# Moving a load of x ahead of the R and V weights in the head of a fused convolution and channel-mix kernel

One core of a Trainium2 chip. The metric is the time of one execution in microseconds of device time (us), lower is better.

## The reference

The kernel computes two layers, one after the other, on x of shape 8 x 4160 x 192 (fp32):

```python
# 1: causal convolution, 7 taps, weights shared by the 24 channels of a head (8 heads)
w = softmax(weight, axis=-1)                       # [8, 7]
y[b, s, h, :] = sum_k w[h, k] * x_pad[b, s + k, h, :]
# 2: channel mix
y_prev = y shifted by one position (zeros first)
xk = mu_k * y + (1 - mu_k) * y_prev
xr = mu_r * y + (1 - mu_r) * y_prev
k  = relu(xk @ w_k)                                # w_k: 192 x 1024
out = sigmoid(xr @ w_r) * ((k * k) @ w_v)          # w_v: 1024 x 192
```

## The kernel before

x is taken two batches at a time, in groups of blocks of 120 positions. A group is loaded to bf16 by a casting DMA from POOL (the GpSimd queue), convolved on the matrix engine (PE) as a product with a banded matrix `toe` that VectorE (DVE) makes from the softmax, copied out of PSUM by ScalarE (ACT), transposed, and mixed on DVE; then K products, ReLU (ACT), square (DVE), R products, sigmoid (ACT), V products, product with the sigmoid (DVE), store. PSUM is one ring of four tiles for everything. The program sets the order on each engine itself (`manual_schedule`). `tails` are two tiles for the last 64 positions of a batch, zeroed on POOL; SP (SyncE) issues the loads of mu.

Only the head changes. Its core, with cuts:

```python
def softmax():
    nc.vector.tensor_reduce(out=w_max, in_=w_raw, ...)     # waits for the attention weights
    ...
    nc.scalar.activation(out=w_exp, in_=w_exp, func=AF.Exp)
    for s in range(2):
        nc.scalar.copy(out=xbs[0][...], in_=x_f32[...])    # first group's x to bf16
    nc.scalar.activation(out=w_sig, ..., func=AF.Sigmoid)  # loads the sigmoid table (1.28 us at 7.56)
    ...

def k_section(ns):                                         # first bundle:
        run(first, 0)                                      # second group's transposes
        warm(k_ps[0], 2)
        for n in ns: k_mm(n, True, True)                   # high 128 channels
        for n in ns: k_mm(n, False, False)                 # low 64 channels
    # ... (the later bundles)

def prologue():
    # ... attention weights and first group's x on the SP and ACT queues
    masks_band()                         # two masks on POOL
    load_x(1)
    load_wk(0, NF // 2)                  # three DMAs
    # ... warm-up products, softmax
    make_toe()
    load_wk(NF // 2, NF)                 # three DMAs
    load_x(2)
    load_wr()                            # five DMAs
    load_wv()
    # ... six tiny loads of mu on the SP queue
    for t in tails:
        nc.gpsimd.memset(t, 0.0)
    conv(0, 0)
    conv(1, 0)
    tr_first()                           # first group's transposes, its mix for K
    x_tile(3, nc.vector)
    load_x(3)                            # fourth group's x
```

Of the kernel before, what the change touches and what calls it, by code (L numbers as in the profile page):

```python
# [14 lines left out]
def kernel(  # L15
# [17 lines left out]
    P = 128  # L33
# [137 lines left out]

    tails = [const.tile([P, 2, 2, P], BF16, tag=f"tail{i}", name=f"tail{i}") for i in range(2)]

    def load_wk(f0, f1):
        fs = slice(f0 * P, f1 * P)
        nc.gpsimd.dma_start(out=wk[:, 0, fs], in_=moe_w_k[0:P, fs])
        nc.gpsimd.dma_start(out=wk[0:LO, 1, fs], in_=moe_w_k[P:D, fs])
        nc.gpsimd.dma_start(out=wk[LO:P, 1, fs], in_=moe_w_k[P:D, fs])

    def load_wr():  # L180
        nc.gpsimd.dma_start(out=wr[:, 0, :], in_=moe_w_r[0:P, :])
        for i in (1, 2):
            nc.gpsimd.dma_start(out=wr[0:LO, i, :], in_=moe_w_r[P:D, :])
        for i in (1, 3):
            nc.gpsimd.dma_start(out=wr[LO:P, i, :], in_=moe_w_r[P:D, :])

    def load_wv():
        nc.gpsimd.dma_start(out=wv, in_=moe_w_v.rearrange("(f p) d -> p f d", p=P))

    def softmax():  # L190
        nc.vector.tensor_reduce(out=w_max, in_=w_raw, axis=mybir.AxisListType.X, op=ALU.max)
        nc.vector.tensor_tensor(
            out=w_exp, in0=w_raw, in1=w_max.unsqueeze(2).to_broadcast([P, H, K]), op=ALU.subtract
        )
        nc.scalar.activation(out=w_exp, in_=w_exp, func=AF.Exp)
        xbs[0] = three.tile([P, GB, 2, D], BF16, tag="xb", name="xb")
        for s in range(2):
            nc.scalar.copy(out=xbs[0][:, : groups[0][2], s, :], in_=x_f32[:, :, s, :])

        nc.scalar.activation(out=w_sig, in_=w_exp[:, 0, 0:1], func=AF.Sigmoid)  # L200
        nc.vector.tensor_reduce(out=w_sum, in_=w_exp, axis=mybir.AxisListType.X, op=ALU.add)
        nc.vector.reciprocal(out=w_sum, in_=w_sum)
        nc.vector.tensor_tensor(
            out=w_nrm,
            in0=w_exp,
            in1=w_sum.unsqueeze(2).to_broadcast([P, H, K]),
            op=ALU.mult,
        )
# [18 lines left out]
    def make_toe():  # L227

        m = mod8[:, :]
        nc.vector.tensor_tensor(  # L230
            out=w_all,
            in0=w_nrm.unsqueeze(2).to_broadcast([P, H, 8, K]),
            in1=bass.AP(tensor=m.tensor, offset=m.offset, ap=[m.ap[0], [0, H], [1, 8], [1, K]]),
            op=ALU.mult,
        )
        with nc.allow_low_precision(reason="a sum of one number and zeros"):
            nc.vector.tensor_reduce(
                out=w_per,
                in_=w_all,
                axis=mybir.AxisListType.X,  # L240
                op=ALU.add,
            )
        for h0, h1 in ((0, 3), (3, H)):
            n = h1 - h0
            nc.vector.tensor_tensor(
                out=toe[:, h0:h1, :].rearrange("p h (c r) -> p h c r", r=8),
                in0=w_per[:, h0:h1, :].unsqueeze(2).to_broadcast([P, n, P // 8, 8]),
                in1=band.rearrange("p (c r) -> p c r", r=8).unsqueeze(1).to_broadcast([P, n, P // 8, 8]),
                op=ALU.mult,
            )  # L250
# [28 lines left out]
    def conv_small(g, copies):  # L279


        nb = groups[g][2]
        ys[g] = [two.tile([P, 4, P], BF16, tag=f"y_small{i}", name="y_small") for i in range(3)]
        tiles = [ring.tile([P, 2, BANK], FP32, tag="k", name="ps_c") for _ in range(2)]
        banks = [t[:, i, 0 : nb * P] for t, i in ((tiles[0], 0), (tiles[1], 0), (tiles[0], 1))]
        for i, o in enumerate(banks):
            o = o.rearrange("p (n s c) -> p n s c", n=nb, s=2 if i == 2 else 1)
            c0, c1 = (P, D) if i == 2 else (0, P)
            for h in range(c0 // G, -(-c1 // G)):
                a, b = max(c0, h * G), min(c1, h * G + G)  # L290
                nc.tensor.matmul(
                    out=o[:, :, :, a - c0 : b - c0],
                    lhsT=toe[:, h, :],
                    rhs=xbs[g][:, :nb, slice(0, 2) if i == 2 else slice(i, i + 1), a:b],
                    start=True,
                    stop=True,
                )
        for i, o in enumerate(banks):
            copies[i](out=ys[g][i][:BLK, :nb, :].rearrange("p n c -> p (n c)"), in_=o[:BLK, :])
# [140 lines left out]
    def k_mm(n, hi, start):  # L440


        s, j = slots[n]
        L = steps[s][2]
        xk = xks[s]
        if start and n not in k_ps:
            k_ps[n] = ring.tile([P, 2, BANK], FP32, tag="k", name="ps_k")
        ps = k_ps[n]
        nf = STEP // L

        for f in range(nf):
            fs = slice((j * nf + f) * P, (j * nf + f + 1) * P)
            for i in range(2):
                r = slice(0, P) if hi else slice(i * LO, (i + 1) * LO)
                nc.tensor.matmul(  # L455
                    out=ps[:, i, f * L : (f + 1) * L],
                    lhsT=wk[r, 0 if hi else 1, fs],
                    rhs=xk[r, i if hi else 2, :L],
                    start=start and f == 0,
                    stop=not start and f == nf - 1,  # L460
                )

    def k_section(ns):

        s, _ = slots[ns[0]]
        if steps[s][2] == TAIL:
            return k_mm_tail(ns[0], steps[s][0])
        if ns[0] == 0:

            k_ps[0] = ring.tile([P, 2, BANK], FP32, tag="k", name="ps_k")  # L470
            run(first, 0)
            warm(k_ps[0], 2)
            for n in ns:
                k_mm(n, True, True)
            for n in ns:
                k_mm(n, False, False)
            return
        h = len(ns) // 2 if ns[0] > 2 else len(ns)
        for n in ns[:h]:
            k_mm(n, True, True)  # L480
        for n in ns[:h]:
            k_mm(n, False, False)
        for n in ns[h:]:
            k_mm(n, False, True)
        for n in ns[h:]:
            k_mm(n, True, False)
# [150 lines left out]
    def conv(g, c):  # L637
        if g < 3:
            act_, dve_ = nc.scalar.copy, nc.vector.tensor_copy
            return conv_small(g, (act_, dve_ if g < 2 else act_, act_))  # L640
        conv_mm(g, c)
        for k in range(c, min(c + 2, len(chunks(g)))):
            conv_out(g, k, nc.scalar.copy)
# [53 lines left out]
    def run(table, b):  # L697
        for fn, a in table.get(b, ()):
            fn(*a)

    def warm(ps, n):
        for i in range(n):
            nc.tensor.matmul(out=ps[:, i % 2, :], lhsT=ones_t, rhs=zeros, start=True, stop=True)

    def prologue():
        nc.sync.dma_start(
            out=w_raw,
            in_=bass.AP(tensor=weight.tensor, offset=weight.offset, ap=[[0, P], [K, H], [1, K]]),
        )
        nc.vector.memset(x_f32[0:32, 0, :, :], 0.0)  # L710
        nc.vector.memset(ones_t, 1.0)
        load_x_first(0, nc.sync)
        load_x_first(1, nc.scalar)
        nc.scalar.preload_act_table(AF.Exp)
        nc.vector.memset(zeros, 0.0)
        x_tile(1, nc.vector)
        nc.gpsimd.affine_select(
            out=ident,
            in_=ones_t,
            pattern=[[1, P]],  # L720
            compare_op=ALU.is_equal,
            fill=0.0,
            base=0,
            channel_multiplier=-1,
        )
        masks_band()
        load_x(1)
        load_wk(0, NF // 2)

        warm(ring.tile([P, 2, BANK], FP32, tag="k", name="warm"), WARM)  # L730
        x_tile(2, nc.vector)
        nc.vector.memset(wr[:, 2:4, :], 0.0)
        masks_mod8()
        softmax()
        make_toe()
        load_wk(NF // 2, NF)
        load_x(2)
        load_wr()
        load_wv()
        for i, m in enumerate((moe_mu_k, moe_mu_r)):  # L740
            nc.sync.dma_start(out=mu[:, i, 0:1], in_=m[0:P])
            nc.sync.dma_start(out=mu[0:LO, i, 1:2], in_=m[P:D])
            nc.sync.dma_start(out=mu[LO:P, i, 1:2], in_=m[P:D])
        for t in tails:
            nc.gpsimd.memset(t, 0.0)
        conv(0, 0)
        conv(1, 0)
        tr_first()
        x_tile(3, nc.vector)
        load_x(3)  # L750

    with tc.manual_schedule():
        prologue()
# [52 lines left out]
```

## Time and profile before

| | |
|---|---|
| timed runs before the change was tried | 445.12, 445.36, 445.37 us |
| the profiled execution | 447.0 us, span 445.3 us, mean granted clock 0.995 (share of PE's full clock) |
| PE busy | 97% of the span |
| x and weights loaded on the POOL queue until about 37 us | the DMA engines 90% busy or more in 30 of the 32 us from 4 to 36 |

The views that matter are the chain of waits (what released each step), the stretches (busy time by engine and granted clock) and ScalarE's timeline (in brackets the idle time ahead of a piece, and what ended it); the prediction shows their lines.

### The profile page before, as it was taken

The page shows a single profiled execution, that of the slowest core. Times are in us where ns is not written, and L with a number is a line of the kernel's source. Part 1 is how long each engine was busy: PE and PEld are TensorE (multiplying, and loading weights), DVE is VectorE, ACT ScalarE, POOL GpSimd, SP SyncE. Part 2 cuts the span into 40 slices and gives each one's busy share as a digit, 9 for nine tenths or more (in the row PEclk, how much of TensorE's full clock was granted, in tenths as well). Part 3 has the DMA queues.
Part 4 walks back from the last instruction along what each step waited for, and adds up shares of the span by engine and source line. Part 5 has one row for each costly group of instructions (what it writes and reads, how often), then busy time and mean ns, then how long its engine had stood idle before and what let it go on. Part 6 is the DMA issues. An engine that isn't in the chain of part 4 may idle for free.

```text
span 445.3 us, 9733 instructions
## 1 busy us (share of the span) xinstructions
PE 430.9 (97%) x3888; PEld 304.9 (68%) x3951; DVE 388.3 (87%) x700; ACT 354.1 (80%) x461; POOL 47.0 (11%) x69
## 2 busy tenths in 40 slices
PE   7789999999999999999999999999999999999996
PEld 3455766766867766776676776677676677666776
DVE  5969799889988999889989888889988898999973
ACT  5868888888897797888888788888889778777772
POOL 6750001102020100012020010010200000000000
PEclk9989999999999999999999999999999999999999
DMA  8996858989596693294899494466955553421123
GB/s 132 147 188 129 199 147 159 152 200 184 133 205 172 146 204 85 79 206 130 161 214 163 116 228 126 111 99 179 195 144 133 158 124 113 102 82 63 45 72 117
DMA packets 133545, 63.94 MB, mean 144 GB/s; under 512 B 84071, under 2 KB 133499, under 8 KB 133499
## 3 DMA queue, kind: packets, MB, share of 16 engines
q1 hardware_dynamic: 95014, 48.38, 41.0%
q0 software_dynamic: 37696, 14.39, 27.7%
q8 instruction: 31, 0.51, 0.4%
q10 hardware_dynamic: 788, 0.54, 0.4%
q14 instruction: 16, 0.12, 0.1%
HBM read 29.39 MB, written 36.99 MB: 149 GB/s over the span
## 4 chain that ended last, share of the span: by engine, by line
PE 86%; DVE 4%; ACT 3%; DMA 3%; issue 2%; POOL 1%; DVEq 0%; ACTq 0%
PE ps_v L554 37%; PE ps_k L455 36%; PE ps_r L549 4%; PE ps_r L550 4%; PE ps_c L271 4%; DMA xb<-in_x_dram 3%; ACT y L313 2%; DVE k L525 1%; ACT k_sb L506 1%; DVE o_sb L581 1%; PE ps_vt L554 1%; ACT r_sb L571 0%; ACT y L316 0%; DVE xr L436 0%; DVE d L392 0%
## 5 line engine op out<-in xcount | busy, mean ns | idle before, releaser
L506 ACT ACTIVATE k_sb<-ps_k 128x1024 bf16<-128x1024 f32 x260 | 245.9, 1037 | 14.5 <-PE ps_k L455 11.2
L455 PE MATMUL ps_k<-xk,wk 64*128 64x512 bf16 (+3 forms) x994 | 189.3, 375 | 5.8 <-ACT k_sb L506 0.6
L554 PEld LDWEIGHTS <-k 128*128 128x128 bf16 x2048 | 170.9, 98 | 14.4 <-issue 0.3
L554 PE MATMUL ps_v<-wv,k 128*128 128x192 bf16 x2048 | 179.4, 246 | 0.1
L525 DVE TENSOR_TENSOR k<-k_sb 128x1024 bf16<-128x1024 bf16 x256 | 167.9, 685 | 10.3 <-ACT k_sb L506 9.2
L455 PEld LDWEIGHTS <-wk 64*128 64x128 bf16 (+1 forms) x1056 | 67.0, 96 | 102.7 <-issue 58.8
L581 DVE TENSOR_TENSOR o_sb<-ps_v,r_sb 128x768 f32<-128x768 f32 x63 | 60.2, 955 | 23.7 <-PE ps_v L554 23.2
L571 ACT ACTIVATE r_sb<-ps_r 128x768 bf16<-128x768 f32 x64 | 53.1, 830 | 24.8 <-PE ps_r L550 24.8
L313 ACT CAST y<-ps_c 120x480 bf16<-120x480 f32 (+4 forms) x78 | 36.1, 518 | 32.4 <-PE ps_c L271 32.4
L122 POOL DMA_DIRECT2D xb<-in_x_dram x34 | 30.7, 908 | 173.7 <-PE ps_k L455 95.2
L549 PE MATMUL ps_r<-wr,xr 128*128 128x192 bf16 x256 | 47.5, 246 | 0.2 <-DVE o_sb L581 0.2
L550 PE MATMUL ps_r<-wr,xr 128*128 128x192 bf16 x256 | 47.6, 247 | 0.0
L436 DVE TENSOR_TENSOR xr<-xr,yT 128x1024 bf16<-128x1024 bf16 (+1 forms) x66 | 36.2, 549 | 2.3
L436 DVE TENSOR_TENSOR xk<-xk,yT 128x1024 bf16<-128x1024 bf16 (+1 forms) x64 | 35.5, 555 | 2.2
L392 DVE TENSOR_TENSOR d<-yT 128x1536 bf16<-128x1536 bf16 (+4 forms) x38 | 31.7, 835 | 0.1
L271 PE MATMUL ps_c<-xb,toe 128*128 128x480 bf16 (+2 forms) x120 | 28.6, 338 | 2.0 <-DMA xb<-in_x_dram 2.0
L433 DVE TENSOR_SCALAR xk<-d,mu 128x1024 bf16<-128x1024 bf16 (+1 forms) x64 | 27.2, 425 | 1.1
L550 PEld LDWEIGHTS <-xr 128*128 128x128 bf16 x256 | 25.1, 98 | 3.9 <-issue 0.4
L549 PEld LDWEIGHTS <-xr 128*128 128x128 bf16 x256 | 25.0, 98 | 3.5
L433 DVE TENSOR_SCALAR xr<-d,mu 128x1024 bf16<-128x1024 bf16 (+1 forms) x66 | 27.1, 410 | 0.0
L316 ACT CAST y<-ps_c 120x480 bf16<-120x480 f32 (+4 forms) x41 | 18.9, 509 | 8.0 <-PE ps_c L271 8.0
L271 PEld LDWEIGHTS <-toe 128*128 128x128 bf16 x120 | 10.9, 98 | 3.0 <-issue 2.2
(69 smaller groups left out, 89.7 us busy)
## 6 DMA issues: line engine op xcount, KB each, us to landing
out_dram<-o_sb SPq DMA_DIRECT2D x61, 384.0 KB, 2.7
y_dram<-y SPq DMA_DIRECT2D x10, 900.0 KB, 6.9
xb<-in_x_dram POOLq DMA_DIRECT2D x14, 480.0 KB, 8.3
xb<-in_x_dram POOLq DMA_DIRECT2D x6, 432.0 KB, 8.2
xb<-in_x_dram POOLq DMA_DIRECT2D x10, 192.0 KB, 6.4
y_dram<-y SPq DMA_DIRECT2D x3, 450.0 KB, 4.1
y_dram<-y SPq DMA_DIRECT2D x1, 810.0 KB, 5.6
xb<-in_x_dram POOLq DMA_DIRECT2D x2, 384.0 KB, 8.7
```

The source lines that it names most:

```text
L271: nc.tensor.matmul(out=ps[:, :, :, i * G : (i + 1) * G], lhsT=toe[:, h, :], rhs=xbs[g][:, :nb, :, h * G : (h + 1) * G], start=True, stop=True,
L313: copy(out=yh[:, :, :, c0 : c0 + n], in_=ps[:BLK, :, :, 0:n])
L433: nc.vector.tensor_scalar(out=o, in0=d[:, sl, :L], scalar1=mu[:, i, part : part + 1], scalar2=None, op0=ALU.mult)
L436: nc.vector.tensor_tensor(out=o, in0=o, in1=yT[:, sl, c0 : c0 + L], op=ALU.add)
L455: nc.tensor.matmul(out=ps[:, i, f * L : (f + 1) * L], lhsT=wk[r, 0 if hi else 1, fs], rhs=xk[r, i if hi else 2, :L], start=start and f == ...
L506: nc.scalar.activation(out=k_sb, in_=ps.rearrange("p a b -> p (a b)"), func=AF.Relu)
L525: nc.vector.tensor_tensor(out=o, in0=i, in1=i, op=ALU.mult)
L549: nc.tensor.matmul(out=o, lhsT=hi, rhs=wr[:, 0, :], start=True, stop=False)
L550: nc.tensor.matmul(out=o, lhsT=lo, rhs=wlo, start=False, stop=True)
L554: nc.tensor.matmul(out=o, lhsT=k2s[s][:, f, t * P : (t + 1) * P], rhs=wv[:, f, :], start=(f == 0), stop=(f == NF - 1),)
L571: nc.scalar.activation(out=r_sbs[s, j], in_=ps, func=AF.Sigmoid)
L581: nc.vector.tensor_tensor(out=o_sb.rearrange("p (b t) d -> p b (t d)", b=2), in0=v_ps.pop((s, j)), in1=r_sbs.pop((s, j)), op=ALU.mult,)
```

## The change

The intent is to end PE's 2 us wait for the fourth group's x, and to start the first K product earlier. The diff, cut to its core:

```diff
-    def load_wk(f0, f1):                    # halves of the columns, 2 x 3 DMAs
+    def load_wk():                          # all columns, 3 DMAs
     ...
     def load_wr():                          # 5 DMAs become 3
     ...
         nc.scalar.activation(out=w_exp, in_=w_exp, func=AF.Exp)
+        nc.scalar.activation(out=w_sig, in_=w_exp[:, 0, 0:1], func=AF.Sigmoid)
         ... copies of the first group's x ...
-        nc.scalar.activation(out=w_sig, in_=w_exp[:, 0, 0:1], func=AF.Sigmoid)
     ...
     def make_toe():                         # whole w_all, w_per, then toe in 3 + 5 heads
+        hc = -(-P // G)                     # now all three steps for 6 heads, then for 2
     ...
-            run(first, 0)
-            warm(k_ps[0], 2)
+            warm(k_ps[0], 3)
             for n in ns:
                 k_mm(n, True, True)
+            run(first, 0)
             for n in ns:
                 k_mm(n, False, False)
     ...
-            return conv_small(g, (act_, dve_ if g < 2 else act_, act_))
+            return conv_small(g, (act_, dve_ if g == 0 else act_, act_))
     ...
+        load_x(1)
         masks_band()
-        load_x(1)
-        load_wk(0, NF // 2)
+        load_wk()
     ...
-        load_wk(NF // 2, NF)
         load_x(2)
-        load_wr()
-        load_wv()
         ... mu ...
-        for t in tails: ...
         conv(0, 0)
-        conv(1, 0)
         tr_first()
+        conv(1, 0)
         x_tile(3, nc.vector)
         load_x(3)
+        load_wr()
+        load_wv()
+        for t in tails: ...
```

More of the change, by code (lines that the diff above doesn't have):

```diff
@@ L172 @@
     tails = [const.tile([P, 2, 2, P], BF16, tag=f"tail{i}", name=f"tail{i}") for i in range(2)]
-    def load_wk(f0, f1):
-        fs = slice(f0 * P, f1 * P)
-        nc.gpsimd.dma_start(out=wk[:, 0, fs], in_=moe_w_k[0:P, fs])
-        nc.gpsimd.dma_start(out=wk[0:LO, 1, fs], in_=moe_w_k[P:D, fs])
-        nc.gpsimd.dma_start(out=wk[LO:P, 1, fs], in_=moe_w_k[P:D, fs])
+    def load_wk():
+        nc.gpsimd.dma_start(out=wk[:, 0, :], in_=moe_w_k[0:P, :])
+        nc.gpsimd.dma_start(out=wk[0:LO, 1, :], in_=moe_w_k[P:D, :])
+        nc.gpsimd.dma_start(out=wk[LO:P, 1, :], in_=moe_w_k[P:D, :])
     def load_wr():
         nc.gpsimd.dma_start(out=wr[:, 0, :], in_=moe_w_r[0:P, :])
-        for i in (1, 2):
-            nc.gpsimd.dma_start(out=wr[0:LO, i, :], in_=moe_w_r[P:D, :])
-        for i in (1, 3):
-            nc.gpsimd.dma_start(out=wr[LO:P, i, :], in_=moe_w_r[P:D, :])
+        lo = bass.AP(tensor=moe_w_r.tensor, offset=moe_w_r.offset + P * D, ap=[[D, LO], [0, 2], [1, D]])
+        nc.gpsimd.dma_start(out=wr[0:LO, 1:3, :], in_=lo)
+        nc.gpsimd.dma_start(out=wr[LO:P, 1:4:2, :], in_=lo)
     def load_wv():
@@ L229, in make_toe @@
         m = mod8[:, :]
-        nc.vector.tensor_tensor(
-            out=w_all,
-            in0=w_nrm.unsqueeze(2).to_broadcast([P, H, 8, K]),
-            in1=bass.AP(tensor=m.tensor, offset=m.offset, ap=[m.ap[0], [0, H], [1, 8], [1, K]]),
-            op=ALU.mult,
-        )
-        with nc.allow_low_precision(reason="a sum of one number and zeros"):
-            nc.vector.tensor_reduce(
-                out=w_per,
-                in_=w_all,
-                axis=mybir.AxisListType.X,
-                op=ALU.add,
-            )
-        for h0, h1 in ((0, 3), (3, H)):
-            n = h1 - h0
+        hc = -(-P // G)
+        for h0, h1 in ((0, hc), (hc, H)):
+            n = h1 - h0
+            nc.vector.tensor_tensor(
+                out=w_all[:, h0:h1],
+                in0=w_nrm[:, h0:h1, :].unsqueeze(2).to_broadcast([P, n, 8, K]),
+                in1=bass.AP(tensor=m.tensor, offset=m.offset, ap=[m.ap[0], [0, n], [1, 8], [1, K]]),
+                op=ALU.mult,
+            )
+            with nc.allow_low_precision(reason="a sum of one number and zeros"):
+                nc.vector.tensor_reduce(
+                    out=w_per[:, h0:h1, :],
+                    in_=w_all[:, h0:h1],
+                    axis=mybir.AxisListType.X,
+                    op=ALU.add,
+                )
             nc.vector.tensor_tensor(
@@ L743, in prologue @@
             nc.sync.dma_start(out=mu[LO:P, i, 1:2], in_=m[P:D])
+        conv(0, 0)
+        tr_first()
+        conv(1, 0)
+        x_tile(3, nc.vector)
+        load_x(3)
+        load_wr()
+        load_wv()
         for t in tails:
             nc.gpsimd.memset(t, 0.0)
-        conv(0, 0)
-        conv(1, 0)
-        tr_first()
-        x_tile(3, nc.vector)
-        load_x(3)
     with tc.manual_schedule():
```

## The prediction

> **What bounds the kernel now.** I read the page first, then the chain that ended last over the first 40 us, then the waits over the rest, then stretches with the granted clock, then ScalarE's timeline.
>
> The page says that the matrix engine is busy nearly everywhere but in the first two slices, 22 us:
>
> ```profile
> span 445.3 us, 9733 instructions
> PE 430.9 (97%) x3888; PEld 304.9 (68%) x3951; DVE 388.3 (87%) x700; ACT 354.1 (80%) x461; POOL 47.0 (11%) x69
> PE   7789999999999999999999999999999999999996
> ```
>
> All that the change touches is over by about 31 us. From 36 us on the waits view, asked for PE alone, has two lines, together 0.8 us in over 400: what is won or lost at the head should go through to the end at about one to one.
>
> ```profile
> PE ps_k L455 <- ACT y L313: 0.6, 1, 0.6
> PE ps_r L549 <- DVE o_sb L581: 0.2, 1, 0.2
> ```
>
> So the question is the head alone. The chain of waits, cut to 12 to 37 us (start, duration, what):
>
> ```profile
> 14.32 0.59 POOL tail L745
> 14.91 0.34 issue
> 15.25 0.58 POOL xb L122
> 15.83 0.35 issue
> 16.18 7.10 DMA xb<-in_x_dram
> 23.28 0.14 issue
> 23.41 0.98 PE ps_c L271 x8
> ...
> 28.43 0.69 ACT k_sb L506
> 29.12 0.22 issue
> 29.34 1.04 ACT k_sb L506
> 30.38 0.04 issue
> 30.42 2.80 PE ps_v L554 x32
> ```
>
> The reader is to see that the fourth group's x, issued on POOL at 15.25 behind two memsets of the tails, lands at 23.28, and that its convolution (L271) starts only then. After it the chain hangs on ScalarE's ReLU, which frees the PSUM tile for the first V product.
>
> The stretches view shows what that wait also does to the clock (columns: PE, PE load, DVE, ACT, POOL busy, granted clock, DMA, GB/s):
>
> ```profile
> 21.40:23.40 2.00, 0.00 (x0) 0.02 (x1) 1.97 (x5) 1.63 (x2) 1.59 (x3) 1.00 1.45 170
> 23.40:24.74 1.34, 1.33 (x15) 1.30 (x16) 1.31 (x4) 0.72 (x2) 1.34 (x2) 1.00 1.53 176
> 24.74:28.16 3.42, 3.42 (x16) 1.14 (x14) 2.12 (x5) 2.65 (x6) 1.05 (x3) 0.50 1.60 193
> ```
>
> PE is empty for 2.0 us and then runs 3.42 us at half clock: its waiting costs twice.
>
> ScalarE's timeline tells how much of this is worth anything (start, busy, what, idle before):
>
> ```profile
> 14.12 3.77 ACT L506 ACTIVATE k_sb<-ps_k 128x1024 bf16<-128x1024 f32 x4 [2.19 <-PE ps_k L455]
> 17.75 1.60 ACT L299 CAST y_small<-ps_c 120x512 bf16<-120x512 f32 x3
> 19.17 3.86 ACT L506 ACTIVATE k_sb<-ps_k 128x1024 bf16<-128x1024 f32 x4
> 24.02 1.35 ACT L313 CAST y<-ps_c 120x480 bf16<-120x480 f32 x3 [0.99 <-PE ps_c L271]
> ...
> 27.51 3.77 ACT L506 ACTIVATE k_sb<-ps_k 128x1024 bf16<-128x1024 f32 x4 [0.77 <-PE ps_k L455]
> ```
>
> From 14.12 to 23.03 ScalarE has no gap: it, and not PE, sets the pace there. It then idles 0.99 us for the late convolution and 0.77 us for the K products at half clock.
>
> [...] The trace has one such stretch of 3.42 us; the window before it, 21.33 to 24.74, was 41% busy (1.4 of 3.41 us)[...]. [...] the trace has 1283 ns for the second one, at 7.56. [...] the two 480 KB loads of the fifth group land at 25.8 and 28.5, which is 2.7 us for 480 KB with packets of 384 bytes, and these queues are 90% busy or more from 16 to 36 us. I use the measured rate, about 180 KB a us.
>
> **The change, part by part.**
>
> 1. *x of the fourth group ahead of R and V weights.* Now 144 KB of R and 384 KB of V stand before it, and the tails' memsets[...]. After: groups two and three (384 KB each), K (512 KB), then this x (480 KB). The third group landed at 14.6 (issue 10.1 plus 4.5); 480 KB more at 180 KB a us is 2.7 us, so 17.3 us instead of 23.28. Its convolution cannot be wanted before about 20.9 (part 4). The wait of 2.0 us on PE and the 0.99 us on ScalarE go. With no gap I expect the half clock to go too, and with it the 0.77 us of ScalarE. Sum on the path: 1.76 us.
>
> 2. *Who pays: R and V.* Bytes in front of R grow by 480 KB: landing 15.7 plus 2.7 is about 18.4; first use 24.1 now, about 22.6 then. V: 18.6 plus 2.7 is 21.3; first use 30.4 now, about 28 then. Both have some 4 to 6 us to spare. The fifth group's x has the same bytes in front of it as before, and its issue on POOL comes no later; landing at 28.5 or earlier, use at 33.1 minus 2.4.
>
> 3. *Fewer loads.* K in 3 instead of 6 issues, R in 3 instead of 5. Bytes are the same; POOL saves 5 issues of about 0.57 us, and the third group's x no longer waits for a free semaphore (1.75 and 0.27 us before its two issues). It shortens a stream that is bound by the DMA engines: nothing on the path by itself.
>
> 4. *First transposes ahead of the second convolution; toe by heads; sigmoid table early.* Now: first K product at 12.72, first ReLU at 14.12. After, in steps. The table load moves to 5.3, ahead of the two casts of x, so the casts end at 8.0 instead of 7.54; the first convolution starts at 8.13 anyway, behind the warm-up products. Six heads of the toe matrix: 0.62 and 0.62 us times 6/8, plus about 0.6 for 768 elements, ready at 7.7; the last two by 8.4, used at 8.9. ScalarE's first copy then starts at 8.5 instead of 8.97 and its second ends at 9.6; the nine transposes (0.64 us) end at 9.95 instead of 10.94. On DVE: yT copy 0.50, difference 0.43, mix 0.75, from 9.6: the first K product at about 11.4, 1.3 us earlier. But the start of the ReLU gets less: the eight K products take about 1.0 us (12.4), then the second group's transposes, now between the halves, 0.8 us (13.2, their inputs are cast on ScalarE by 12.0), then the low halves 0.45 us: ReLU at 13.65, 0.5 us earlier. The low half also needs the last mu load, which landed at 12.4 (5.76 plus 6.6), and the K weights (12.5): no limit at 13.2, but close. Worth 0.5 us.
>
> 5. *Copies.* The second group's third copy moves from DVE (0.69 us) to ScalarE, ahead of the first ReLU: in ScalarE's idle 2.19 us, free. One warm-up product more, in a gap: free.
>
> Sum: 0.5 at the first ReLU, 0.99 before the casts, 0.77 before the third set of ReLUs: 2.26. A second way to the same place: after, ScalarE is full from 13.65. Until the casts: 8.91 us of work, 22.55; casts and sigmoid 2.73 us, 25.3; two ReLUs and the third, ending 2.85 us later, free the tile of the V product: about 28.1 instead of 30.42, 2.3 us earlier. From there on PE is full. 445.36 minus 2.3 is 443.1; I say 443.0, as the DMA stream also loses its stall at 14.5 to 16.
>
> **Rivals.**
>
> *A: PE's loss is the measure.* PE idles 2.0 us, loses about 1.7 us at half clock, and starts 1.3 us earlier: up to 5 us, 440.4. Against it: ScalarE's gapless run from 14.12 to 23.03 stands in between, with all four PSUM tiles in its hands. I give it little.
>
> *B: the K weights, in fewer and larger loads, or mu, become the new wait.* The high part of K now brings all 1024 columns before any low part. If low parts land at 13 or later, part 4 gives nothing: 443.6. For it: everything lands 5.8 to 6.4 us after issue in that crowded stretch. Against: 512 KB are the same bytes, issued from about 4.1 as now.
>
> *C: the gap merely moves.* PE, held back by ScalarE, waits in crumbs of 0.3 to 0.6 us between 17 and 23 us; if one window is still half idle, the clock drops anyway, costing the 0.77 us: 443.8. Or R's landing slips beyond 22.6. Against: PE had 4.53 us of work in 16.0 to 21.4 and kept its clock.
>
> *D: hidden anyway.* If later slack absorbed the head, 445 stays. Against it: 0.8 us of PE waits after 36 us.
>
> **Range and chances.** Centre 443.0. B and C together would give 444.2; half of A's extra gives 441.8. Eight in ten: 441.8 to 444.2. Two per cent is 8.9 us, more than the head's idle PE time outside the warm-up; so faster by over 2%: 0.01; within 2%: 0.98; slower by over 2%: 0.01, as no wait that I can see grows.
>
> **What would show each step.** Part 1: no wait of L270 (the fourth group's convolution) for a DMA; granted clock 1.00 from 21 to 30 us; ScalarE without gaps before its casts and its third set of ReLUs. Part 2: no wait of R or V products for a DMA. Part 4: first K product near 11.4, first ReLU near 13.65. The sum: the first V product at about 28.1. The prediction is wrong if PE gains waits after 36 us, if the clock still halves between 17 and 30 us, or if the first ReLU isn't earlier than 14.12.

Where the text is marked as cut it told of the hardware what no trace or run of this case shows, or gave a count that no view of the profile shows. The sum is 0.5 plus 0.99 plus 0.77, or 2.26 us, which makes 443.1 of 445.36 and was told as 443.0, and its rate of 180 KB a us is read from the trace. "One such stretch" is the one at half clock (granted 0.50 from 24.74 to 28.16), and "the second one" is ScalarE's second table load, ahead of the sigmoid (ACT_TABLE_LOAD, 1.28 us from 7.56). That another window so empty would cost the clock again, on which rival C rests, was inference from this one stretch.

## The result

Changed: 445.5 us median (445.29 to 445.67, 4 runs), before: 445.24 (444.41 to 445.37, 4 runs). The ratio is 1.001, 95% interval 0.9992 to 1.0027: no change that these runs can tell, and 1.3 us above the top of the predicted range.

Yet the profile of the changed kernel has a span of 443.8, against 445.3 in the profile of before. Its chain of waits, cut to the first 40 us (start, duration, what):

```profile
0.80 4.54 DMA w_raw<-in_weight_dram
5.36 0.22 DVE w_max L189
...
8.03 0.56 DVE toe L244
...
12.70 1.03 PE ps_k L454 x8
...
29.06 2.80 PE ps_v L553 x32
```

ScalarE's timeline of the changed kernel:

```profile
14.73 3.77 ACT L505 ACTIVATE k_sb<-ps_k 128x1024 bf16<-128x1024 f32 x4 [1.38 <-PE ps_k L454]
...
19.77 3.86 ACT L505 ACTIVATE k_sb<-ps_k 128x1024 bf16<-128x1024 f32 x4
23.40 1.48 ACT L312 CAST y<-ps_c 120x480 bf16<-120x480 f32 x3
...
25.94 3.98 ACT L505 ACTIVATE k_sb<-ps_k 128x1024 bf16<-128x1024 f32 x4
```

And its stretches, for the same times as before's:

```profile
21.40:23.40 2.00, 1.59 (x20) 1.22 (x18) 1.97 (x7) 2.00 (x3) 0.90 (x2) 1.00 1.58 189
...
24.74:28.16 3.42, 3.24 (x28) 1.62 (x27) 2.74 (x6) 3.42 (x7) 1.06 (x2) 1.00 1.27 143
```

The wait, ScalarE's two gaps and the half clock are gone, as predicted. But the first ReLU comes at 14.73, not at 13.65: 0.6 us later than before, where 0.5 us earlier was expected. The chain starts with the attention weights, which the softmax reads at 5.36 us; before, at 4.49 (there the chain ran through the second group's x instead). Two questions are open: what delays the start, and why a profile that is 1.5 us shorter goes with times that are no shorter.

**Theory 1: the start gives the gain back.** The second group's x, now issued on POOL ahead of the band masks, delays the small loads on the other queues; its toe matrix, and all that follows, comes later. The first profile of before is typical.

**Theory 2: the first profile of before is odd.** At 447.0 us it isn't what the timed runs do. In those there is no half clock and next to no wait for x, so there was nothing to gain.

### The profile page after: what moved, and what is told of

Same layout as the page of the kernel before. It is cut to its first block, busy times and chain, and to the rows that moved or that the text cites. A ratio compares the mean times of both kernels' runs of the same rounds, so it can differ in the third digit from the quotient of the medians.

```text
span 443.8 us, 9795 instructions
## 1 busy us (share of the span) xinstructions
PE 433.2 (98%) x3952; PEld 304.2 (69%) x3952; DVE 388.0 (87%) x701; ACT 354.5 (80%) x462; POOL 44.6 (10%) x64
## 4 chain that ended last, share of the span: by engine, by line
PE 89%; DVE 5%; ACT 3%; DMA 2%; issue 1%; DVEq 0%; ACTq 0%
PE ps_v L553 38%; PE ps_k L454 37%; PE ps_r L548 4%; PE ps_r L549 4%; PE ps_c L270 4%; DVE k L524 2%; ACT y L312 1%; DMA w_raw<-in_weight_dram 1%; ACT k_sb L505 1%; PE ps_vt L553 1%; DVE d L391 1%; DMA xb<-in_x_dram 1%; ACT r_sb L570 0%; DVE xk L435 0%; DVE o_sb L580 0%
## 5 line engine op out<-in xcount | busy, mean ns | idle before, releaser
L454 PE MATMUL ps_k<-xk,wk 64*128 64x512 bf16 (+3 forms) x1056 | 191.9, 373 | 1.8 <-ACT y L312 0.3
L432 DVE TENSOR_SCALAR xk<-d,mu 128x1024 bf16<-128x1024 bf16 (+1 forms) x64 | 27.0, 422 | 1.1
L432 DVE TENSOR_SCALAR xr<-d,mu 128x1024 bf16<-128x1024 bf16 (+1 forms) x66 | 27.1, 411 | 0.0
```

What stands on the lines that cost most here:

```text
L432: nc.vector.tensor_scalar(out=o, in0=d[:, sl, :L], scalar1=mu[:, i, part : part + 1], scalar2=None, op0=ALU.mult)
L454: nc.tensor.matmul(out=ps[:, i, f * L : (f + 1) * L], lhsT=wk[r, 0 if hi else 1, fs], rhs=xk[r, i if hi else 2, :L], start=start and f == ...
```

## The experiments

All kernels below gave correct results. They ran on three occasions, the first two on one chip and the third on another; each set is compared with the runs of before beside it.

### First set: which part does what

**The kernel before, unchanged.** No edit.

> The kernel before, unchanged, to get a second profile of it and its spread. Theory 1 (the start gives it back: early x of the second group delays the small attention weights by 0.9 us, and that eats the gain of the fourth group's early x; the first profile of before is typical): time 445.2, span 445.3 or so in the profile, half clock after the gap before the fourth group's convolution. Theory 2 (that profile is of an odd execution: 447.0 us against 445.1 to 445.4 of its timed runs): time 445.2, profiled span 443.4 to 443.7, granted clock 0.998 or more, no half clock between 17 and 30 us.

Measured: 445.33 us (before beside it: 445.14; ratio 1.0001, 0.9987 to 1.0015). The profiled span is 443.0, clock 1.0. ScalarE's timeline in this second profile of before:

```profile
13.91 3.77 ACT L506 ACTIVATE k_sb<-ps_k 128x1024 bf16<-128x1024 f32 x4 [2.18 <-PE ps_k L455]
...
18.96 3.86 ACT L506 ACTIVATE k_sb<-ps_k 128x1024 bf16<-128x1024 f32 x4
22.64 1.43 ACT L313 CAST y<-ps_c 120x480 bf16<-120x480 f32 x3
...
25.20 3.91 ACT L506 ACTIVATE k_sb<-ps_k 128x1024 bf16<-128x1024 f32 x4
```

and, of its waits on PE in the first 40 us, the one for the fourth group's convolution:

```profile
PE ps_c L271 <- ACT k_sb L506: 0.8, 1, 0.8
```

The same program, with none of the gaps. The convolution of the fourth group starts at 22.03 after waiting 0.8 us, put down to a ReLU that frees PSUM; ScalarE goes from the second set of ReLUs to the casts without a stop. The load was issued 0.2 us earlier than in the first profile and its second half landed 5.9 us after issue instead of 7.1. Theory 2 is right about before.

**Changed kernel, second group's x late again.**

```diff
-        load_x(1)
         masks_band()
+        load_x(1)
         load_wk()
```

> The changed kernel with the second group's x issued after the band masks again, as before. Theory 1: the attention weights land at 4.5 us instead of 5.3, the first K product comes 0.6 to 0.9 us earlier, time 444.6 to 444.9. Theory 2 alone: landing at 5.3 as in the changed kernel, time 445.5.

Measured: 445.12 us, ratio 0.9992 (0.998 to 1.0005) to before; span 443.0. The waits view (who, for whom: us in total, times, longest) on the attention weights, in the changed kernel and in this one:

```profile
DVE w_max L189 <- DMA w_raw<-in_weight_dram: 2.8, 1, 2.8
```

```profile
DVE w_max L189 <- DMA w_raw<-in_weight_dram: 2.0, 1, 2.0
```

They land 3.7 us after issue again. In the traces this edit is worth 0.8 us (443.0 against 443.8). The first K product comes at 11.84, 0.7 us earlier than in before's second profile and 0.9 us earlier than in its first, where part 4 said 1.3; the first ReLU comes at 13.94, not earlier at all. The second group's convolution waits for no load although its x is late: in the new order the first transposes stand ahead of it. The time lies between the two theories' numbers. Theory 1 has the cause of the late start, and a further question appears: what holds the ReLU.

**Kernel before, fourth group's x early and nothing else.**

```diff
         load_x(2)
-        load_wr()
-        load_wv()
         ... mu ...
-        for t in tails: ...
         conv(0, 0)
         conv(1, 0)
         tr_first()
         x_tile(3, nc.vector)
         load_x(3)
+        load_wr()
+        load_wv()
+        for t in tails: ...
```

> The kernel before with only one part of the change: the fourth group's x issued ahead of the R and V weights and of the memsets of the tails. Theory 1: 443.7 to 444.0, 1.3 to 1.6 us less than before. Theory 2: the timed runs of before pay little for that wait, so 445.0 to 445.3.

Measured: 445.05 us, ratio 0.999 (0.9977 to 1.0002); span 443.1 against 443.0 for the kernel before beside it. The convolution starts at 21.08 instead of 22.03; the casts behind it at 22.62 instead of 22.64. In the traces the main part of the change is worth nothing in an ordinary execution, since ScalarE is not free before 22.6. The timed runs alone leave more room: the interval reaches down to a gain of 1.0 us.

**Changed kernel, fourth group's x late again** (the reverse edit, on the changed kernel).

```diff
         load_x(2)
+        load_wr()
+        load_wv()
         ... mu ...
+        for t in tails: ...
         conv(0, 0)
         tr_first()
         conv(1, 0)
         x_tile(3, nc.vector)
         load_x(3)
-        load_wr()
-        load_wv()
-        for t in tails: ...
```

> The changed kernel with only this part undone: the fourth group's x again behind the R and V weights and the tails. Theory 1: 446.8 to 447.2. Theory 2: 445.5 to 446.0.

Measured: 445.42 us, ratio 0.9999 (0.9987 to 1.0012); span 443.6, first ReLU 14.57, attention weights read at 5.21. No gap before the casts. Theory 1 had 446.8 or more; theory 2's 445.5 is 0.1 off.

### Second set: what delays the weights, what holds the ReLU

**Kernel before, second group's x early and nothing else.**

```diff
-        masks_band()
         load_x(1)
+        masks_band()
         load_wk(0, NF // 2)
```

> The kernel before with one part of the change alone: the second group's x issued ahead of the two band masks. If this is what delays the attention weights: their landing 4.4 to 4.6 us after issue instead of 3.7, first ReLU at 14.5 to 14.7 instead of 13.91, profiled span 443.6 to 443.8. If something else in the change does it: landing at 3.7, first ReLU 13.9, span 443.0.

Measured: 445.09 us (before beside it: 445.06), ratio 1.0004 (0.999 to 1.0018). In the profile the attention weights land 4.7 us after issue instead of 3.7, so this edit alone does it. The first ReLU comes at 14.26, later by 0.35 and not by the 0.6 to 0.8 expected: the convolution of the second group, which waited 0.5 us for its x in before, now doesn't. The span is 443.9, of which 0.5 us is a wait of ScalarE for the fourth group's x, which again landed late; this profile was the slowest of the kernel's four runs (445.78; the others 444.85 to 445.18). So the later landing is shown, and its price in the old order isn't told apart from nothing by the timed runs.

How it comes about, the stretch from 3.5 to 4.5 us tells in part (columns as in the prediction; the last two are DMA share and GB/s), first in before, then in the changed kernel:

```profile
3.50:4.50 1.00, 1.00 (x4) 0.41 (x3) 0.01 (x1) 0.26 (x1) 1.00 (x2) 1.00 0.92 302
```

```profile
3.50:4.50 1.00, 1.00 (x4) 0.40 (x3) 0.00 (x0) 0.26 (x1) 0.93 (x3) 1.00 0.60 192
```

In that microsecond only the packets of the SP and ACT queues are moving, in both kernels; with the POOL load issued 0.6 us earlier they move at 192 instead of 302 GB/s, before a single packet of the POOL load is recorded. It is not that a packet takes longer (33.5 ns in the mean, 32.0 before): there are 286 instead of 460, so the DMA engines stand idle between them (60% busy, 92% before). Why they do, the trace doesn't show. The weights land 3.6 to 3.8 us after issue in six profiles with this x late, 4.4 to 4.7 us in four with it early. Over ten profiles with this x late, the softmax reads its weights at 4.46 to 4.92 us, over four with it early at 5.21 to 5.57.

**What holds the first ReLU.** In the changed kernel with the second group's x late, VectorE's timeline has a wait between the first K product and the ReLU:

```profile
...
12.96 0.49 DVE L411 SCALAR_TENSOR_TENSOR xk<-d,mu,yT 128x256 bf16<-128x256 bf16 x1 [0.98 <-DMA mu<-in_moe_mu_k_dram]
```

The low part of the mix waits 0.98 us for a load of 64 numbers, issued at 5.7 us and landed 7.2 us later. On PE, the second group's transposes (0.80 us from 12.71) stand before the low products too. Two edits, apart and together:

```diff
             for n in ns:
                 k_mm(n, True, True)
-            run(first, 0)
             for n in ns:
                 k_mm(n, False, False)
+            run(first, 0)
```

> The changed kernel with the second group's x late, and the second group's transposes after the low half of the first K products instead of between the halves. Theory mu (the low half waits for the last mu load, which lands near 12.9): first ReLU 13.9 as without it, span 443.0. Theory transposes (their 0.8 us on the matrix engine hold up the low half): first ReLU 13.2 to 13.5, span 442.3 to 442.6.

Measured: 445.65 us, ratio 1.0014 (1.0001 to 1.0028), span 443.8: slower. The attention weights came at 4.92 in this profile, so read from the first K product: 12.25, the mix waits 0.72 us for mu, ReLU at 14.09, that is 1.84 us after the first K product instead of 2.10. Mu holds it, as its theory said. The span is another matter: 0.4 us of the loss is the weights' (4.92 against 4.51), and PE now waits 1.09 us for VectorE's mix of the second step, of which the next runs say more.

```diff
         load_x(1)
+        load_mu(0, moe_mu_k, nc.gpsimd)     # mu for K: three loads, POOL queue
         load_wk()
     ...
-        ... six loads of mu on the SP queue ...
+        load_mu(1, moe_mu_r, nc.sync)
```

> The changed kernel with the second group's x late, and the three loads of mu for K on the POOL queue ahead of the K weights. Theory mu: low mix of the first step at 12.0 to 12.3 instead of 12.96, first ReLU 13.3 or earlier. Theory transposes: the low mix comes early, the first ReLU stays at 13.8 to 13.9, span 442.9.

Measured: 444.76 us, ratio 0.9997 (0.9981 to 1.0012), span 442.8. The low mix runs at 11.97, 1 us earlier; the ReLU stays at 14.01, since the transposes now fill the time. Each wait hides behind the other.

```profile
11.97 0.49 DVE L411 SCALAR_TENSOR_TENSOR xk<-d,mu,yT 128x256 bf16<-128x256 bf16 x1
...
14.01 3.77 ACT L505 ACTIVATE k_sb<-ps_k 128x1024 bf16<-128x1024 f32 x4 [1.57 <-PE ps_k L454]
```

The edit also has a price: the K weights are now issued 1.6 us later, their first load lands at 11.9, and the first K product waits for it until 11.97 (11.84 without the edit).

Then both edits together:

> Both of the last two edits. If both waits hold the first ReLU: first ReLU 13.0 to 13.3. If the end then follows the first ReLU at 429.05 us, as in all profiles so far but the first: span 442.1 to 442.4. If VectorE's chain for the second step (yT copy, difference, mix) is the next bound, its start 0.4 us later takes the gain back: span 442.8 to 443.0.

Measured: 445.47 us, ratio 1.0014 (1.0002 to 1.0027), span 443.6. The first ReLU comes at 13.71, the earliest of all, and the kernel is slower. PE's timeline shows why (first K products, transposes, K products of the second step):

```profile
11.98 1.91 PE L454 MATMUL ps_k<-xk,wk 128*128 128x256 bf16 x16 [0.30 <-DVE xk L411]
13.82 0.81 PE L348 MATMUL ps_t<-ident,y_small 120*128 120x120 bf16 x12
...
18.45 0.82 PE L454 MATMUL ps_k<-xk,wk 128*128 128x512 bf16 x3 [1.61 <-DVE xk L435]
```

The transposes start 1.1 us later than with neither edit (13.82 against 12.71), and behind them hangs the whole second step: copy, difference, two mixes on VectorE. PE waits 1.61 us for it and ScalarE 0.59 before its second set of ReLUs, at 19.85 instead of 18.99. Not all of that is the order. From the first to the second set of ReLUs it is 5.05 us with neither edit, 5.64 with the transposes moved alone (`a_trafter`) and 6.14 here; the extra 0.5 us is one instruction of the mix on VectorE (L432, from 16.67), which took 1.00 us here against 0.48 to 0.62 in the other versions of the changed kernel. Why it did isn't shown. The instruction in `a_trafter`, then here:

```profile
17.05 0.49 DVE L432 TENSOR_SCALAR xk<-d,mu 128x1024 bf16<-128x1024 bf16 x1
```

```profile
16.67 1.00 DVE L432 TENSOR_SCALAR xk<-d,mu 128x1024 bf16<-128x1024 bf16 x1
```

The third hypothesis is right in kind: VectorE's chain is the next bound. Its size was told too small (443.0 at most), by about that 0.5 us. The first ReLU at 13.71 missed the 13.0 to 13.3 as the low K products waited for the last K weights, which landed at about 13.2. With that, the law "the end is the first ReLU plus 429 us", which had held for five profiles, falls; what held in all kernels where the fourth group's x was no wait is the second set of ReLUs plus 424 us (423.7 to 424.1 in all eleven profiles of that kind, counting those below).

### Third set: the odd profile

**Kernel before, fourth group's x later still.**

```diff
         x_tile(3, nc.vector)
+        for _ in range(2):                  # four more memsets of 0.55 us on POOL
+            for t in tails:
+                nc.gpsimd.memset(t, 0.0)
         load_x(3)
```

> The kernel before with four more memsets of the tails (0.55 us each) ahead of the fourth group's x: its load is issued 2.2 us later, to make by force what the first profile of before had by chance. If the wait and the half clock after it made that profile slow: PE idle 2 to 3 us before the fourth group's convolution (at 24.0 to 24.4), a stretch of 3.4 us at half clock within 21 to 31 us, span 445.2 to 446.0. If the wait costs only itself: no half clock, ScalarE idle about 1.5 us before the casts, span 444.4 to 444.8. If it's hidden anyway: 443.0.

Measured: 446.24 us (445.79 to 446.81) against 444.95, ratio 1.0028 (1.0015 to 1.0042); span 444.7. Waits on PE in the first 36 us and two pieces of ScalarE's timeline:

```profile
PE ps_c L271 <- DMA xb<-in_x_dram: 2.1, 1, 2.1
```

```profile
19.51 3.77 ACT L506 ACTIVATE k_sb<-ps_k 128x1024 bf16<-128x1024 f32 x4 [0.39 <-PE ps_k L455]
24.41 1.35 ACT L313 CAST y<-ps_c 120x480 bf16<-120x480 f32 x3 [1.12 <-PE ps_c L271]
```

PE waits 2.1 us, as in the first profile of before, and the end moves by ScalarE's 1.1 us, plus 0.4 us of another wait, that before 19.51: while the added memsets ran, VectorE's first mix instruction of the second step took 2.25 us (0.49 in the other profiles of the old order). There is no half clock (granted 1.00 in every stretch from 19 to 30 us): "the wait costs only itself". In the two traces of the comparison the changes of the granted clock lie on a grid: in the first profile of before its records begin at 7.68 (full), 24.74 (0.50), 28.16 (full) and 444.58 us (0.50), that is 5, 1 and 122 steps of 3.413 us apart, and in the changed kernel's at 6.23 and 443.14, 128 such steps apart. So the stretches were taken on each trace's own grid, in this kernel and in the first profile of before:

```profile
19.89:23.30 3.41, 1.83 (x20) 1.03 (x16) 3.34 (x10) 3.40 (x4) 1.09 (x2) 1.00 1.18 130
```

```profile
21.33:24.74 3.41, 1.40 (x17) 1.31 (x16) 3.34 (x8) 2.42 (x4) 2.93 (x4) 1.00 1.47 171
```

The step with PE busy 54% kept the clock, the one with 41% lost it. So a gap of 2.1 us left the clock full in this execution and one of 2.0 us was followed by half clock in the other; the grid fell differently in the two (at 23.30 and at 21.33). Counted on its own grid, each of the two traces of the comparison has 128 whole steps from where its clock is first full. The 253 with PE busy 62% or more (the least 2.12 of 3.41 us, in the changed kernel from 6.23) were followed by full clock, the other three by half clock: the one with 41% (1.40 us), and the last of each trace, with 15% (0.52 us, before, from 441.17) and 13% (0.43 us, changed, from 439.72). Where between 41% and 54% the limit lies, and whether the busy share is all that counts, isn't shown.

**Kernel before, third profile.**

> The kernel before once more, for a third profile. If the first one was an exception: span 443.0 to 443.3, convolution of the fourth group at 22 us or earlier than the second set of ReLUs ends, no half clock. If it is a coin toss: 445.

Measured: 444.75 us (one execution), span 443.0, no half clock, casts at 22.66. With the timed runs beside it (nine runs, spans 443.0 to 443.5) the first profile was an exception. It wasn't the only long execution, though: in the first set one of before's took 446.43 us (span 444.7) and one 445.93 (444.2), both at full clock; no trace tells why.

**Changed kernel again.**

> The changed kernel once more, beside before on the same chip. If the traces are right (443.76 against 443.0), it is 0.3 to 0.8 us slower than before in its timed runs too; attention weights land at 5.2 us or later, first ReLU at 14.5 to 14.8.

Measured: 445.33 us against 444.95, ratio 1.0015 (1.0002 to 1.0029): slower by 0.4 us in the medians (the ratio's mean takes in the long run named next). Span 443.6, weights read at 5.22, first ReLU 14.59. One of its five runs took 446.78 us with a mean clock of 0.996. By an estimate one step of 3.41 us at half clock makes about that of the mean (1 less half of 3.41 over its span of 445.1 us); no trace of it was kept, so where it fell isn't known.

**Second group's x late, mu for K on POOL, again.**

> The version with the second group's x late and mu for K on the POOL queue, once more. It is the best span so far, 442.8; expected 0.2 to 0.4 us faster than before, which is within what timed runs can tell, at best.

Measured: 444.47 us against 444.95, ratio 0.9989 (0.9977 to 1.0002), span 442.7. It is the best version found, by 0.5 us in the medians, and its interval just includes 1.

The milestones side by side (us from the start of the span; from the timelines):

| | before, first profile | before, second | changed | changed, second group's x late | that and both edits |
|---|---|---|---|---|---|
| softmax reads its weights | 4.49 | 4.57 | 5.36 | 4.51 | 4.65 |
| first K product | 12.72 | 12.51 | 12.70 | 11.84 | 11.98 |
| first ReLU | 14.12 | 13.91 | 14.73 | 13.94 | 13.71 |
| second set of ReLUs | 19.17 | 18.96 | 19.77 | 18.99 | 19.85 |
| casts of the fourth group | 24.02 | 22.64 | 23.40 | 22.61 | 23.49 |
| third set of ReLUs | 27.51 | 25.20 | 25.94 | 25.15 | 26.35 |
| first V product | 30.42 | 28.24 | 29.06 | 28.27 | 29.26 |
| end | 445.3 | 443.0 | 443.8 | 443.0 | 443.6 |

## Why the prediction was wrong

It said 443.0 us, 441.8 to 444.2; 445.5 was measured. "Within 2%" was right and says little for a change in the head of a long kernel.

**The step that failed first is the base of the sum: "445.36 minus 2.3 is 443.1".** The 2.3 us were read off an execution of 447.0 us, and taken from a time of other executions. The span of 445.3 looked like the time of 445.36, but time is span plus 1.7 us; a timed run of 445.3 has a span of 443.6, 0.6 us above that of the profiles without the gaps (443.0), so there is no room in it for gaps of 2 us. Taken from its own execution the sum would have been 447.0 minus 2.3, or 444.7. This is 1.6 of the 2.5 us. The rest is mainly part 4, which lost 0.6 us where it was to win 0.5, less some 0.3 us that part 1 won beyond its sum; with the measured terms, 447.0 minus 2.1 plus 0.6 is the 445.5 measured. It could have been seen: the clock of 0.995 and the 447.0 stood with the profile.

**Part 1** (0.99 for the casts and 0.77 for the third ReLUs, 1.76 in all). The mechanism was right for the odd execution: between its first and second profile before differs by 0.21 us at the first ReLU, 1.17 more at the casts (1.38 in all) and 0.93 more at the third ReLUs (2.31). That is 2.10 for wait and clock. In an ordinary execution the term measured 0 in the traces: early x alone left 443.1 of 443.0. Rival D, "hidden anyway", is what happened, though not by slack later: ScalarE, which the prediction itself named as pace-setter, isn't ready for that convolution before 22.6 us, and x lands at 21.9. One thing is to be added to the rate: the 180 KB a us count the bf16 bytes that the loads write; by the types of the tiles they read fp32, twice as many. It did serve, as it was used on like loads: x of the fourth group landed at 16.8 (told 17.3).

**Part 2** (R and V have time) held: no R or V product of the changed kernel waits for a load, and R landed by 18.2 and V at 21.0 (told 18.4 and 21.3). **Parts 3 and 5** held as far as the traces show: nothing on the path.

**Part 4** (0.5 us earlier at the first ReLU) failed by its sign: 0.6 later in the profiles compared, 0.8 later than in before's second. Two terms were wrong. The prediction took 4.5 us for the attention weights from before's trace and gave no thought to what an earlier POOL load does to the loads beside it: plus 0.8. None of its parts names the edit that does it, the second group's x ahead of the band masks, and nothing in the new order waits for that load even when it is late. (By-heads toe was right: it was sized as 7.7 and 8.4 us, 3.2 and 3.9 after the weights, and took 3.2, 8.59 less 5.36, and 4.0.) The other term is the way to the ReLU. With the weights on time, the first K product came at 11.84 as against "about 11.4" (the sum starts VectorE's copy at 9.6, before the transposes that it ends at 9.95; it started at 10.00), and the ReLU at 13.94 as against 13.65. Rival B, mu as the new wait, is there at 0.98 us, where the text had "no limit at 13.2, but close". The last K weights, B's other half, landed at 12.7, just ahead of mu. The transposes stand behind mu and would hold the ReLU to 14.0 by themselves.

**The second route** (ScalarE full from the first ReLU; V 14.45 us after it) was right: 14.33 measured. Its starting point was off. **Rival A** had been given little, rightly. **Rival C**, in its second half (the clock drops anyway), did not occur in the changed kernel's two profiles; a run with a clock of 0.996 suggests that it can. **The range** was too narrow by its own terms: 443.6 for B and 443.8 for C make 444.4 together, not 444.2; 445.5 lies outside either.

What stays open: why the other queues moved 192 instead of 302 GB/s from 3.5 to 4.5 us with the POOL load issued early, before its first packet; why an instruction of VectorE's mix took 1.00 us in one profile; how often before's x comes late enough to matter (in one of its three profiles, and in the only one of the kernel that differs from it in the second group's x alone; timed runs keep no trace); and whether the changed kernel's early load of the fourth group is worth having as insurance against that.

## What to carry to other kernels

Before you subtract anything from a time, check that the profiled execution is one of the kind that you timed: compare its own time and clock with the timed runs', and keep span and time apart. A wait on one engine is worth only what the next engine in line was idle for (here 2.0 us of PE and 0.99 us of ScalarE), and that has to be read in a typical execution (where it was nothing). Moving one load earlier can move others later (here one by 0.6 us, another by 0.8 us); and where two waits lie on one another, ask what the third chain does before you remove both.
